# The set-up of a fused FFT and MLP-mixer kernel: sine tables by a masked scale, x folded by landed halves, and a new order with fillers on TensorE

## Chip, cores, metric

One NeuronCore of a Trainium2 chip runs the whole program. The metric is the device time of one execution in microseconds. The profile comes from one of the timed executions; its span is about 1.8 us shorter than the reported time. On one core every run counts as "fast", but the granted TensorE clock (the share of full speed that the chip allowed) differs in the set-up from run to run. Each run comes with its mean clock only. As a scale, estimated from the clock records of the traces: one stretch of 3.4 us at half clock lowers the mean by 0.0028, and a low clock at the very end of the program by up to 0.0019 more. So 0.998 to 1.000 means no low stretch in the set-up, 0.996 or 0.997 one, 0.993 or 0.994 two, 0.990 to 0.992 three.

## The reference

```python
def reference(x, w_tok1, w_tok2, w_ch1, w_ch2):      # x: 8 x 3008 x 256, float32
    x = np.fft.fft(np.fft.fft(x, axis=1), axis=2).real
    xt = x.transpose(0, 2, 1)
    h = np.maximum(xt @ w_tok1, 0.0) @ w_tok2        # token MLP, width 256
    u = x + h.transpose(0, 2, 1)
    h2 = np.maximum(u @ w_ch1, 0.0) @ w_ch2          # channel MLP, width 1536
    return u + h2
```

## The kernel before

The kernel builds its own sine tables while the first batch of x loads. For batch 0 the order of work is: fold x with its mirror (`xm`, two gathers) on VectorE; products `pz` with a small sine table and their copies `z`; products `pw` with the feature table `tdu`/`tdb` and their copies `w`; the token tables `tp` and `tq` are made by ScalarE sines, turned on TensorE (`tts_p`, `tts_q`) and multiplied into the token weights w1 (`ph` products, copies `hp` and `hq`). Then the token MLP of batch 0 and the main stage follow; I call its first channel product (`pc`) the start of the main stage.

The token weights are loaded after x on the same queue:

```python
    x_tiles = {0: load_x(0)}          # four loads of xp, two gathers of xm
    ...
    for i in range(2):
        gdma(w1p[64 * i:64 * i + 64, :, :],
             dram(w1_t, i * DTOK, [[NQ * DTOK, 64], [2 * DTOK, NG], [1, DTOK]]))
        gdma(w1m[64 - 64 * i:128 - 64 * i, 0:NG - 1 + i, :],
             dram(w1_t, (25 - i) * DTOK,
                  [[NQ * DTOK, 64], [2 * DTOK, NG - 1 + i], [1, DTOK]]))
    w2s = const.tile([P, 2, S], FP16, tag="w2s")
    gdma(w2s[:], ...)
```

The tables, the `ph` products, and the order of the set-up:

```python
    def table3(tab, r):                     # tab: 128 x 12 x 128; two quarters of it stay zero
        for i in range(2):
            h = slice(64 * i, 64 * i + 64)
            sin(tab[h, :, h], r[h, :, :], S)

    def carried(tts, dst, g2, e):           # two groups of 12; needs w1p[g] and w1m[11 - g]
        ph = ps_mm("ph")
        for k in range(2):
            g = 2 * g2 + k
            o = ph[:, k * DTOK:(k + 1) * DTOK]
            nc.tensor.matmul(o, lhsT=tts[0][...], rhs=w1p[:, g, :], start=True, stop=False)
            nc.tensor.matmul(o, lhsT=tts[1][...], rhs=w1m[:, NG - 1 - g, :], ...)
        copy(e, dst[...], ph[:])
    ...
    warm(36)                    # warm-up matmuls, 256 columns
    turn(tp, tts_p, 0)          # 12 transposes; the last argument counts filler matmuls (result unused)
    pieces = fold0()
    take(pieces, 1)
    table_d()
    table_perm()
    take(pieces, 4)
    own = zw0()                 # steps: 8 of pz, then 12 of pw
    ...                         # rest of vq on VectorE
    take(own, 3)
    turn_rows(tts_p, 1.0, 0)
    table_b()
    take(own, 5)
    table3(tq, vq)
    take(own, 3)
    carried(tts_p, hp, 0, 1)    # first use of w1
    ...                         # the other pw, five more hp, tq turned
```

## Time and profile before

| | before |
|---|---|
| time, median of 3 | 611.73 us (611.49 to 612.89) |
| run that was profiled | 612.39 us, span 610.6 us, mean clock 0.991 |
| start of the main stage in that run | 39.50 us |

From the page of the profile: span, TensorE's busy time, the granted clock in 40 slices of 15 us (tenths of full speed), and the engines' shares of the chain that ended last.

```profile
span 610.6 us, 15693 instructions
...
PE 594.0 (97%) x6319; PEld 425.0 (70%) x6319; DVE 453.7 (74%) x1017; ACT 441.0 (72%) x988; POOL 147.9 (24%) x232
...
PEclk9699999999999999999999999999999999999999
...
PE 92%; DVE 4%; DMA 1%; ACT 1%; issue 0%; POOL 0%; DVEq 0%; POOLq 0%
...
```

TensorE bounds the kernel, and only the second slice of 40 shows a clock below 90%. The windows view (busy us of each engine and number of instructions, then the granted clock, a share of the DMA engines that I don't use, and GB/s) cuts the set-up into stretches of 3.4 us:

```profile
core 0: us, PE busy (x) PEld busy (x) DVE busy (x) ACT busy (x) POOL busy (x), PEclk, DMA share, GB/s
9.20:12.60 3.40, 1.98 (x19) 1.53 (x18) 2.06 (x8) 3.25 (x6) 2.88 (x5) 1.00 1.10 186
12.60:16.00 3.40, 1.24 (x22) 1.07 (x22) 2.68 (x9) 2.02 (x4) 1.48 (x2) 1.00 1.43 192
16.00:19.40 3.40, 3.40 (x33) 2.13 (x30) 3.40 (x8) 3.00 (x6) 3.23 (x6) 0.50 1.47 198
19.40:22.80 3.40, 2.94 (x24) 2.27 (x22) 2.36 (x6) 2.13 (x4) 2.95 (x9) 0.50 1.14 221
22.80:26.20 3.40, 3.40 (x31) 3.13 (x29) 1.33 (x3) 1.50 (x3) 2.71 (x5) 0.50 1.07 221
...
```

In the stretch before 16.0 us TensorE is busy for 1.24 of 3.40 us; then the clock is 0.50 for three stretches. (The clock's records in a trace begin at its first rise, here at 9.2 us. The views count the time before as full, but the warm-up matmuls of 256 columns start 0.21 us apart in it and 0.11 us apart after it.) From the chain of waits (start, us, what):

```profile
...
5.27 7.93 DMA xm<-in_x_dram,ix
...
15.58 0.40 PE pz L476 x5
...
18.78 1.67 DVE z L293 x3
...
20.50 1.38 PE pw L519 x11
21.88 0.21 PE ph L398
...
39.50 1.42 PE pc L704 x6
...
```

The fold starts when the second gather lands (13.2 us), z is done at 20.45. From the timeline (start, us from the first start to the last end of the merged instructions, engine, instruction, count; in brackets the idle time and what ended it):

```profile
...
3.90 1.67 ACT L140 ACTIVATE tp<-pcol 64x768 f16<-64x768 f32 x2
...
5.58 1.69 ACT L140 ACTIVATE tq<-pcol 64x768 f16<-64x768 f32 x2
...
10.85 1.68 ACT L245 ACTIVATE tp<-vp 64x768 f16<-64x768 f32 x2
...
13.32 0.23 DVE L447 TENSOR_TENSOR xp<-xp,xm 94x16 f16<-94x16 f16 x1 [1.99 <-DMA xm<-in_x_dram,ix]
...
15.07 2.74 POOL L90 TENSOR_SCALAR tdu<-tdu 128x1 f16<-128x1 f16 x2 [1.92 <-ACT tdu L245]
...
21.68 0.42 PE L398 MATMUL ph<-w1p,tt 128*128 128x256 f16 x1
...
21.89 0.42 PE L400 MATMUL ph<-w1m,tt 128*128 128x256 f16 x1
...
```

Four zero fills occupy ScalarE for 3.4 us; the fold waits 1.99 us for the gather; two tiny steps on GpSimd take 2.74 us.

### The profile page before, as it was taken

To read this page: it belongs to the slowest core of one execution; us is meant where nothing else is said; L and a number is where in the kernel's file an instruction comes from. 1 tells how busy PE (TensorE), PEld (TensorE's weight loads), DVE (VectorE), ACT (ScalarE), POOL (GpSimd) and SP (SyncE) were. 2 spreads that over 40 slices of the span, in tenths; PEclk is the share of its full clock that TensorE was granted. 3 is DMA by queue.
4 is the path that set the end of the run, shared out by engine and by line. 5 is a ranking of instruction groups with operands and counts; after the bars stand their busy time and mean duration, and the time that the engine had idled before them with its cause. 6 is when DMAs were issued, how large, how long until landed. Compare 5 with 4: busy or idle time off the path is not lost.

```text
span 610.6 us, 15693 instructions
## 1 busy us (share of the span) xinstructions
PE 594.0 (97%) x6319; PEld 425.0 (70%) x6319; DVE 453.7 (74%) x1017; ACT 441.0 (72%) x988; POOL 147.9 (24%) x232
## 2 busy tenths in 40 slices
PE   4999999999999999999999999999999999999996
PEld 3765667666777677766777777766777667766675
DVE  7669679658987598757988689856979676676572
ACT  8667887686778777777777767777777777767772
POOL 7700413211233112401414211321121112111131
PEclk9699999999999999999999999999999999999999
DMA  9993943824538423682339233383231523342424
GB/s 148 209 178 87 176 83 56 160 44 84 74 66 155 96 53 62 115 131 53 71 70 167 62 77 80 63 184 61 53 66 44 103 53 75 66 70 58 91 58 100
DMA packets 86601, 56.53 MB, mean 93 GB/s; under 512 B 54864, under 2 KB 83472, under 8 KB 85776
## 3 DMA queue, kind: packets, MB, share of 16 engines
q1 hardware_dynamic: 78048, 37.84, 32.5%
q0 software_dynamic: 8256, 17.49, 16.5%
q8 instruction: 49, 0.80, 0.6%
q14 instruction: 24, 0.20, 0.1%
q10 hardware_dynamic: 224, 0.20, 0.1%
HBM read 34.98 MB, written 24.64 MB: 98 GB/s over the span
## 4 chain that ended last, share of the span: by engine, by line
PE 92%; DVE 4%; DMA 1%; ACT 1%; issue 0%; POOL 0%; DVEq 0%; POOLq 0%
PE pc L704 39%; PE px L745 23%; PE py L745 9%; PE pu L664 7%; PE po L802 4%; PE pt L572 4%; PE pz L476 2%; DMA xm<-in_x_dram,ix 1%; PE pq L604 1%; PE py L604 1%; PE pw L519 1%; PE pw L556 1%; DVE sb L721 1%; PE pw L555 1%; DVE w L558 1%; PE ph L400 1%
## 5 line engine op out<-in xcount | busy, mean ns | idle before, releaser
L707 ACT ACTIVATE c<-pc 128x512 f16<-128x512 f32 (+1 forms) x572 | 295.9, 595 | 38.5 <-PE pc L704 20.5
L730 POOL TENSOR_TENSOR osb<-osb,rt 128x256 f32<-128x256 f32 x84 | 80.1, 954 | 384.4 <-DVE osb L730 374.5
L704 PE MATMUL pc<-ut,wc1p 128*128 128x512 f16 x576 | 140.5, 379 | 0.0
L745 PEld LDWEIGHTS <-c 128*128 128x128 f16 x2016 | 121.4, 98 | 20.8 <-issue 1.2
L704 PE MATMUL pc<-ut,wc1m 128*128 128x512 f16 (+1 forms) x576 | 134.9, 370 | 0.0
L672 DVE TENSOR_TENSOR ut<-pu,yt 128x512 f16<-128x512 f32 (+1 forms) x96 | 64.6, 674 | 52.9 <-PE pu L664 52.8
L745 PEld LDWEIGHTS <-sb 128*128 128x128 f16 x1512 | 90.0, 98 | 10.8 <-DVE sb L721 0.7
L750 ACT ACTIVATE m<-px 128x256 f32<-128x256 f32 x126 | 48.5, 385 | 66.6 <-PE px L745 42.9
L704 PEld LDWEIGHTS <-wc1p 128*128 128x128 f16 x576 | 52.1, 98 | 49.2 <-issue 2.6
L704 PEld LDWEIGHTS <-wc1m 128*128 128x128 f16 x576 | 53.0, 98 | 46.4
L745 PE MATMUL px<-wst,c 128*128 128x128 f16 x1008 | 70.8, 219 | 0.2 <-DVE c L721 0.2
L745 PE MATMUL px<-wc,c 128*128 128x128 f16 x1008 | 63.1, 219 | 0.0
L295 ACT ACTIVATE z<-pz 128x480 f16<-128x480 f32 (+1 forms) x59 | 39.7, 673 | 17.7 <-PE pz L476 11.9
L721 DVE TENSOR_TENSOR sb<-sb,c 128x768 f16<-128x768 f16 x84 | 50.3, 598 | 2.9
L730 DVE TENSOR_TENSOR osb<-py,m 128x256 f32<-128x256 f32 x84 | 35.1, 418 | 22.2 <-ACT m L750 17.4
L664 PE MATMUL pu<-w2p,uu 128*128 128x512 f16 (+1 forms) x168 | 50.0, 379 | 0.0
L721 DVE TENSOR_TENSOR sb<-c 128x768 f16<-128x768 f16 x84 | 48.1, 573 | 2.4 <-ACT c L707 2.4
L721 DVE TENSOR_TENSOR sb<-c,sb 128x768 f16<-128x768 f16 x84 | 47.1, 561 | 0.0
L721 DVE TENSOR_TENSOR c<-c 128x768 f16<-128x768 f16 x84 | 46.5, 554 | 0.0
L558 DVE SCALAR_TENSOR_TENSOR w<-alt,pw 128x131 f16<-128x131 f16 x84 | 29.3, 350 | 19.7 <-ACT w L295 19.1
L611 DVE TENSOR_TENSOR yt<-py,qs 128x512 f16<-128x512 f32 x48 | 30.9, 686 | 16.1 <-ACT qs L607 15.8
L745 PE MATMUL py<-wst,sb 128*128 128x128 f16 x504 | 35.2, 219 | 0.5 <-DVE sb L721 0.5
(187 smaller groups left out, 696.2 us busy)
## 6 DMA issues: line engine op xcount, KB each, us to landing
out_dram<-osb SPq DMA_DIRECT2D x83, 256.0 KB, 3.8
xp<-in_x_dram POOLq DMA_DIRECT2D x16, 272.0 KB
out_dram<-osb SPq DMA_DIRECT2D x11, 192.0 KB, 3.2
xp<-in_x_dram POOLq DMA_DIRECT2D x16, 127.5 KB
rt<-ut SPq DMA_TRANSPOSE x96, 3.5
w2s<-in_moe_w_tok_dram POOLq DMA_DIRECT2D x1, 1504.0 KB
w1p<-in_moe_w_tok_dram POOLq DMA_DIRECT2D x2, 384.0 KB
wc<-in_moe_w_ch_dram POOLq DMA_DIRECT2D x1, 768.0 KB
```

What stands on the lines that cost most here:

```text
L295: nc.scalar.activation(out=out_, in_=in_, func=AFT.Copy)
L558: nc.vector.scalar_tensor_tensor(out=w[:, g, 0:131], in0=alt[:], scalar=pw[:, 131:132], in1=pw[:, 0:131], op0=AT.mult, op1=AT.add)
L572: nc.tensor.matmul(pt[:, o:o + n], lhsT=hw[:, g, th * P:th * P + P], rhs=w[:, g, f:f + n], start=(g == 0), stop=(g == NG - 1))
L611: nc.vector.tensor_tensor(out=yt[:, h, CW * c:CW * c + CW], in0=py[:], in1=qs[:], op=op)
L664: nc.tensor.matmul(pu[:, 0:n], lhsT=uu[:, th, int(minus), h, :], rhs=w2_cols(b, c)[:, th], start=(th == 0), stop=(th == 1))
L672: nc.vector.tensor_tensor(out=ut[:, h, 0:n].rearrange("p (a b) -> p a b", b=64), in0=pu[:, 0:n].rearrange("p (b a) -> p a b", b=64), in1=y ...
L704: nc.tensor.matmul(pc[:, 0:n], lhsT=wc[:, h, ct * P:(ct + 1) * P], rhs=ut[:, h, 0:n], start=(h == 0), stop=(h == 1))
L707: nc.scalar.activation(out=c1[:, ct, 0:n], in_=pc[:, 0:n], func=AFT.Relu)
L721: nc.vector.tensor_tensor(out=o, in0=x, in1=y, op=op)
L730: eng.tensor_tensor(out=o, in0=x, in1=y, op=AT.add)
L745: nc.tensor.matmul(o[:, t], lhsT=a(k)[:, f:f + P], rhs=w(k), start=(first and t == 0 and k == 0), stop=(k == HC - 1), skip_group_check=True)
L750: nc.scalar.activation(out=m[:, i], in_=pa[:, 0], func=AFT.Copy)
```

## The change

Its intent: the quarters of tp and tq that must be zero come out of the sine itself, by a scale vector that is 0 on half the partitions; rounding for vp goes from VectorE to ScalarE and the two tiny steps from GpSimd to VectorE; the first half of the fold needs only the first gather; and the order on TensorE, with more fillers, should leave no idle spell long enough to halve the clock.

```diff
-    for t in (tp, tq):
-        for i in range(2):
-            h = slice(64 * i, 64 * i + 64)
-            nc.scalar.activation(
-                out=t[h, :, 64 - 64 * i:128 - 64 * i],
-                in_=pcol[h, :].unsqueeze(2).to_broadcast([64, NG, 64]),
-                func=AFT.Copy, scale=0.0)
...
     def table3(tab, r):
         for i in range(2):
-            h = slice(64 * i, 64 * i + 64)
-            sin(tab[h, :, h], r[h, :, :], S)
+            nc.scalar.activation(out=tab[:, :, 64 * i:64 * i + 64], in_=r[:],
+                                 func=AFT.Sin, scale=half[i][:])
...
+    near(vp, mp)
+    half = pvec("half0"), pvec("half1")
+    ts(half[0][:], icol[:], -PI2 / S, AT.mult, PI2 / S, AT.add)
+    ts(half[1][:], icol[:], PI2 / S, AT.mult)
...
-        tt(out=xp[:, 1:NR, 0], in0=xp[:, 1:NR, 0], in1=xm[0:KR, ::-1, 0], op=add)
...
+        for t0 in (13, 9, 5, 1):
+            if t0 in (13, 5):
+                mirror(t0 - 4, t0 + 4, 0, 1)
+            mirror(t0, t0 + 4, 1, D)
...
-    Z0_ORDER = ((11, (0, 1)), (0, (1, 1)), (6, (0, 1)), (1, (0, 1)))
-    W0_COPY = [1] * 5 + [0, 1, 0, 1, 0, 1, 0]
+    Z0_ORDER = ((11, (0, 0)), (0, (1, 1)), (6, (0, 1)), (1, (0, 1)))
+    W0_COPY = [1] * 5 + [0, 1, 1, 1, 0, 1, 0]
...
-    warm(36)
-    turn(tp, tts_p, 0)
+    warm(24)
+    near(vq, mq)
+    table_d()
     pieces = fold0()
-    take(pieces, 1)
...
+    take(pieces, 5)
+    own = zw0()
+    filler(8)
+    take(own, 2)
+    turn(tp, tts_p, 8)
+    take(own, 2)
+    table_b()
+    rest_of(vq, mq, S)
+    take(own, 4)
+    turn_rows(tts_p, 1.0, 0)
+    table3(tq, vq)
     table_perm()
...
     take(own, 3)
     carried(tts_p, hp, 0, 1)
```

More of the change, by code (lines that the diff above doesn't have):

```diff
@@ L285, in filler @@
     def filler(n):
-        pw = ps_out("filler")
+        pw = ps_mm("filler")
         for _ in range(n):
@@ L307 @@
     ts(gp[:], jrow[:, 0:NG], r2[:], AT.mult, offp[:], AT.add)
-    nc.vector.memset(altu[:], 1.0)
-    for f in (2, 132):
-        nc.vector.memset(altu[:, f:f + 127:2], -1.0)
     nc.vector.scalar_tensor_tensor(
@@ L314, with near, rest_of @@
         op0=AT.mult, op1=AT.add)
-    ixc = const.tile([P, 1], I32, tag="ixc")
-    cfeat = pvec("cfeat")
-    ts(cfeat[:], pcol[:], 1.0, AT.is_lt, -128.0, AT.mult)
-    ts(cfeat[:], cfeat[:], 256.0, AT.add)
-    nc.vector.tensor_tensor(out=ixc[:], in0=cfeat[:], in1=pcol[:], op=AT.subtract)
-    for o, i, scale, bias in ((mq, mp, 1.0, dq), (vq, mq, 1.0 / S, up),
-                              (vq, vq, 1.0, down)):
-        nc.scalar.activation(out=o[:], in_=i[:], func=AFT.Identity, scale=scale,
-                             bias=bias[:])
+    nc.vector.memset(altu[:], 1.0)
+    for f in (2, 132):
+        nc.vector.memset(altu[:, f:f + 127:2], -1.0)
+    def near(v, m):
+        for i, scale, bias in ((m, 1.0 / S, up), (v, 1.0, down)):
+            nc.scalar.activation(out=v[:], in_=i[:], func=AFT.Identity, scale=scale,
+                                 bias=bias[:])
+    def rest_of(v, m, period):
+        nc.vector.scalar_tensor_tensor(out=v[:], in0=v[:], scalar=-float(period),
+                                       in1=m[:], op0=AT.mult, op1=AT.add)
+    near(vp, mp)
+    half = pvec("half0"), pvec("half1")
+    ts(half[0][:], icol[:], -PI2 / S, AT.mult, PI2 / S, AT.add)
+    ts(half[1][:], icol[:], PI2 / S, AT.mult)
     mask0, q24 = pvec("mask0"), pvec("q24")
@@ L338 @@
     nc.scalar.activation(out=t0h[:], in_=cs[0:NQ, 0:4:2, :], func=AFT.Copy, scale=0.5)
-    reduced(vp[:], vp[:], mp[:], S)
+    rest_of(vp, mp, S)
     table3(tp, vp)
+    nc.scalar.activation(out=mq[:], in_=mp[:], func=AFT.Identity, bias=dq[:])
     ident = const.tile([P, P], FP16, tag="ident")
@@ L351 @@
     nc.vector.tensor_copy(out=t1b[:, 0:3:2, :], in_=t1n[:, :, 0, :])
+    ixc = const.tile([P, 1], I32, tag="ixc")
+    cfeat = pvec("cfeat")
+    ts(cfeat[:], pcol[:], 1.0, AT.is_lt, -128.0, AT.mult)
+    ts(cfeat[:], cfeat[:], 256.0, AT.add)
+    nc.vector.tensor_tensor(out=ixc[:], in0=cfeat[:], in1=pcol[:], op=AT.subtract)
+    nc.vector.scalar_tensor_tensor(out=md[:], in0=vd[:], scalar=-256.0, in1=md[:],
+                                   op0=AT.mult, op1=AT.add)
     td0 = const.tile([P, 131], FP16, tag="td0")
@@ L358, in table_d, with table_b @@
     def table_d():
-        nc.vector.scalar_tensor_tensor(out=md[:], in0=vd[:], scalar=-256.0, in1=md[:],
-                                       op0=AT.mult, op1=AT.add)
         sin(tdu[:, 2:130], md[:, 0:128], 256)
         sin(tdu[:, 132:WD], md[:, 128:255], 256)
+    def table_b():
         for f, s in ((1, 0.5), (130, -0.5)):
-            ts(tdu[:, f:f + 1], tdu[:, 129:130], 0.5, AT.mult, s, AT.add, eng=pl)
-    def table_b():
+            ts(tdu[:, f:f + 1], tdu[:, 129:130], 0.5, AT.mult, s, AT.add)
         nc.vector.tensor_tensor(out=tdb[:], in0=tdu[:], in1=altu[:], op=AT.mult)
@@ L446, in fold0, with mirror @@
         tt, add = nc.vector.tensor_tensor, AT.add
-        tt(out=xp[:, 1:NR, 0], in0=xp[:, 1:NR, 0], in1=xm[0:KR, ::-1, 0], op=add)
+        def mirror(t0, t1, lo, hi):
+            rv = slice(16 - t0, 16 - t1 if t1 < 17 else None, -1)
+            rd = slice(D - lo, D - hi if lo else None, -1) if lo else 0
+            c = slice(lo, hi) if lo else 0
+            t = slice(t0, t1)
+            tt(out=xp[:, t, c], in0=xp[:, t, c], in1=xm[0:KR, rv, rd], op=add)
         r = slice(0, NQ)
-        for t0, t1 in ((13, 17), (9, 13), (5, 9), (1, 5)):
-            t = slice(t0, t1)
-            rv = slice(16 - t0, 16 - t1 if t1 < 17 else None, -1)
-            tt(out=xp[:, t, 1:D], in0=xp[:, t, 1:D], in1=xm[0:KR, rv, D - 1:0:-1], op=add)
+        for t0 in (13, 9, 5, 1):
+            if t0 in (13, 5):
+                mirror(t0 - 4, t0 + 4, 0, 1)
+            mirror(t0, t0 + 4, 1, D)
             yield
@@ L840, in take @@
             next(g, None)
-    warm(36)
-    turn(tp, tts_p, 0)
+    warm(24)
+    near(vq, mq)
+    table_d()
     pieces = fold0()
-    take(pieces, 1)
-    table_d()
-    table_perm()
-    take(pieces, 4)
-    own = zw0()
-    nc.vector.scalar_tensor_tensor(out=vq[:], in0=vq[:], scalar=-float(S), in1=mq[:],
-                                   op0=AT.mult, op1=AT.add)
-    take(own, 3)
-    turn_rows(tts_p, 1.0, 0)
-    table_b()
-    take(own, 5)
-    table3(tq, vq)
+    take(pieces, 5)
[9 more added lines that the diff above has]
+    table3(tq, vq)
+    table_perm()
     take(own, 3)
@@ L860 @@
     carried(tts_p, hp, 1, 0)
-    take(own, 1)
+    take(own, 2)
+    carried(tts_p, hp, 2, 1)
     turn(tq, tts_q, 0)
     take(own, 2)
-    carried(tts_p, hp, 2, 1)
+    carried(tts_p, hp, 3, 1)
     turn_rows(tts_q, -1.0, 0)
-    take(own, 2)
-    carried(tts_p, hp, 3, 1)
-    take(own, 2)
+    take(own, 3)
     carried(tts_p, hp, 4, 0)
```

## The prediction

> **What bounds it now.** The page shows TensorE busy 97% of 610.6 us, and the chain of waits is 92% TensorE. The change touches only the set-up, the first 31 us; later work keeps its order on every engine, so at most the start of the main stage (first channel product, 39.5 us in the chain) moves. The chain of set-up: the second gather of mirrored x lands at 13.2 us; VectorE folds x in four blocks until 16.7; casts of z end at 20.45, and the first full run of pw products starts at 20.50; from there TensorE, with copies to VectorE and ScalarE, sets the pace to 31 us.
>
> The windows view gives the granted clock: 1.00 until 16.0, 0.50 from 16.0 to 26.2, then 1.00. Before the drop TensorE was busy only 1.25 of 3.41 us (idle 1.42 us before the transposes of tp and 2.16 us before pz). The Trainium skill, "TensorE: Matmul & The Clock Gate", Part 1, says that a free-running window of about 3.4 us decides the clock. This trace fits: half speed lasts 10.2 us, three windows. In the halved stretch a pw matmul of 128 columns starts every 0.11 us, later every 0.056.
>
> **What the change does.**
> - Removes four ScalarE zero fills (0.84 us each, 3.36 in all). The sines grow from 64 to 128 partitions at the same 768 columns, so 0.84 us each as before.
> - Moves two passes of vp (0.55 + 0.69 us) from VectorE to ScalarE (two of 0.94), and two tiny GpSimd steps (1.4 us each) to VectorE (0.15 each, estimate).
> - Folds the first two blocks after the first gather alone. The gathers are issued 1.7 us apart; I estimate it lands near 11.2 us. Fold ends near 14.8 instead of 16.7.
> - Puts pz before the tp transposes, defers the reversed rows and the tq sines, adds 16 filler matmuls, and takes 12 of 36 warm-up matmuls away, which also start 0.95 us later (mp comes first).
>
> By hand, with the trace's durations: tdu sines end 14.0; first pz 13.4; z complete near 19.1, against 20.45. Gain 1.3 us. Then the first ph product may wait for w1, which lands near 21 us (w2s, next in the queue, lands at 28.4 after about 7.5 us of bytes). If the clock is full there, 2.9 us of halved matmul time goes away, but the copies take over: about 5.5 us each on VectorE and ScalarE after 21 us, so the last hp copy ends near 27.3, against 30.8 to 31.3. All set-up gain passes to the end, because w2s (28.4) and wc1 land before they are needed.
>
> So: clock full, about -3.5 us; clock halved again, about -1.3. The second is a real chance: I expect TensorE idle from 10.6 to 13.4, and again about 1.4 us before pw, and 24 cold warm-up matmuls (0.213 us each, 5.1 us) need not fill one free-running window. I give full clock two chances in three.
>
> **Predicted: 608.7 us**, range 606.8 to 610.6 (before 611.73). Faster by over 2% 1%, within 2% 98.5%, slower 0.5%.
>
> **What would show it.** Windows view: granted clock 1.00 from 16 to 26 us. Timeline: first fold near 11.2 with the releaser a DMA, first pz near 13.4, z done near 19, last hp copy near 27.3. Main stage of unchanged length, starting near 36 instead of 39.5. ScalarE's fills absent.
>
> **What would make it wrong.** The two gathers landing together at 13.2 (the fold then gains nothing); the clock halving at 12.6 or 16 after all, or never rising after the shorter warm-up; w1 landing later than 21 us; ScalarE, which now has the vq passes and the tdu sines just before the z copies, becoming the bound; or loads of the next batch colliding differently and giving the gain back at the first channel products.

## The result

| | before | changed |
|---|---|---|
| time, median of 4 | 611.81 us (611.49 to 612.89) | 612.26 us (611.57 to 612.66) |
| ratio of fast runs | | 1.0003 (0.9986 to 1.002) |
| profiled run | 612.39 us, span 610.6 | 611.57 us, span 609.8 |
| start of the main stage | 39.50 us | 38.72 us |

Ratios here and below are the mean time of one kernel's fast runs over that of the other's of the same rounds, so they are not quite the ratio of the medians. The predicted 3 us did not come, and the measured median lies above the predicted range. The profiled run of before is one of its slower ones, that of the changed kernel is its fastest of four, so the 0.8 us between the two profiles is no gain of the medians.

The page of the changed kernel:

```profile
span 609.8 us, 15701 instructions
...
PEclk9899999999999999999999999999999999999999
...
```

The windows view, the same stretches:

```profile
...
9.20:12.60 3.40, 2.56 (x19) 1.82 (x17) 3.33 (x16) 3.33 (x5) 3.10 (x4) 1.00 1.14 197
12.60:16.00 3.40, 3.15 (x57) 2.86 (x58) 2.51 (x8) 3.40 (x8) 3.04 (x6) 1.00 1.45 195
16.00:19.40 3.40, 1.68 (x16) 0.93 (x15) 2.92 (x6) 3.40 (x7) 2.98 (x7) 1.00 1.51 208
19.40:22.80 3.40, 1.25 (x10) 0.97 (x9) 0.99 (x3) 0.80 (x1) 2.50 (x5) 0.78 1.07 214
22.80:26.20 3.40, 3.40 (x39) 3.09 (x38) 2.16 (x5) 1.31 (x3) 0.00 (x0) 0.72 1.05 218
...
```

The recorded clock is now full from its first rise (11.1 us) until 21.3 us. But TensorE is busy for only 1.68 us and 1.25 us of the third and fourth stretch, and the clock then falls after all. The chain of waits says why:

```profile
...
8.68 12.91 DMA w1m<-in_moe_w_tok_dram
...
21.64 0.37 PE ph L403
22.01 0.21 PE ph L401
...
38.72 1.42 PE pc L714 x6
...
```

The gather of x and the fold have left the chain, and so have z and the first pw products. In their place stands one line of 12.91 us: the load of w1m, from its issue to its landing at 21.6 us. The timeline shows the same on TensorE:

```profile
...
8.71 1.76 ACT L242 ACTIVATE tp<-vp,half 128x768 f16<-128x768 f32 x2 [0.29 <-DVE vp L315]
...
10.95 0.77 DVE L456 TENSOR_TENSOR xp<-xp,xm 94x8 f16<-94x8 f16 x2
...
12.85 0.60 PE L486 MATMUL pz<-t1n,xp 94*128 94x96 f16 x10 [1.09 <-DVE xp L456]
...
15.53 0.39 DVE L90 TENSOR_SCALAR tdu<-tdu 128x1 f16<-128x1 f16 x2
...
19.22 0.27 PE L401 MATMUL ph<-w1p,tt 128*128 128x256 f16 x1
...
21.64 0.37 PE L403 MATMUL ph<-w1m,tt 128*128 128x256 f16 x1 [2.15 <-DMA w1m<-in_moe_w_tok_dram]
...
```

The pieces of the change did as intended: no zero fills, sines on 128 partitions at 1.76 us for two (1.68 on 64), the fold starts at 10.95 without a wait instead of 13.32, the first pz is at 12.85 instead of 15.58. "ScalarE: Activation LUTs", Step-by-step, in the Trainium skill states that scale may be a per-partition operand. A single sine took 0.93 to 0.97 us with it on 128 partitions, against 0.83 with one scale for all on 64; the prediction had 0.84 "as before". What each of the two differences costs was not separated. The first product with w1p starts at 19.22, 2.5 us earlier than before. The next instruction needs w1m and waits 2.15 us; TensorE takes its instructions in order, so all the later pw products, which need nothing more, stand behind it. The first w1m product starts at 21.64, against 21.89 before: a gain of 0.25 us. And behind the wait the clock is low: the chain has 0.21 us for each `ph` product, where at full clock it has 0.11.

From the start of the main stage to the end the two kernels take the same: 610.6 - 39.5 = 571.1 and 609.8 - 38.7 = 571.1 us. In all the runs below this lies between 570.9 and 571.3 (in halves_w_first_filled the chain does not pass the first pc; by its start on TensorE, 35.05, it is 571.4), so the start of the main stage tells a profiled run's worth, and the loss must be looked for in front of it.

### The profile page after: what moved, and what is told of

It reads as the page before. It is cut to its first block, busy times and chain, and to the rows that moved or that the text cites. A ratio compares the mean times of both kernels' runs of the same rounds, so it can differ in the third digit from the quotient of the medians.

```text
span 609.8 us, 15701 instructions
## 1 busy us (share of the span) xinstructions
PE 591.3 (97%) x6323; PEld 423.0 (69%) x6323; DVE 453.2 (74%) x1020; ACT 439.4 (72%) x986; POOL 147.8 (24%) x230
## 4 chain that ended last, share of the span: by engine, by line
PE 92%; DVE 3%; DMA 2%; ACT 1%; POOL 1%; issue 0%; DVEq 0%; POOLq 0%
PE pc L714 39%; PE px L755 23%; PE py L755 9%; PE pu L674 7%; PE po L812 4%; PE pt L582 4%; DMA w1m<-in_moe_w_tok_dram 2%; PE pz L486 1%; PE pq L614 1%; PE py L614 1%; PE pw L566 1%; PE pw L565 1%; DVE sb L731 1%; DVE w L568 1%; PE ph L403 0%; DVE osb L740 0%
## 5 line engine op out<-in xcount | busy, mean ns | idle before, releaser
L288 ACT ACTIVATE z<-pz 128x480 f16<-128x480 f32 (+1 forms) x60 | 40.0, 671 | 16.9 <-PE pz L486 11.0
L621 DVE TENSOR_TENSOR yt<-py,qs 128x512 f16<-128x512 f32 x48 | 30.9, 686 | 16.0 <-ACT qs L617 15.7
```

Source lines behind the costliest of these rows:

```text
L288: nc.scalar.activation(out=out_, in_=in_, func=AFT.Copy)
L621: nc.vector.tensor_tensor(out=yt[:, h, CW * c:CW * c + CW], in0=py[:], in1=qs[:], op=op)
```

## The experiments

Theory A: the change shortens the way to the first w1 product, but w1m lands at 21.6 us whatever the engines do. Before was already within about 0.3 us of that landing (if w1m landed then as in the changed kernel: its own trace shows no wait, so it only says that the load was in by 21.89, and in before_filled below it came later). The wait takes the gain, and the idle in it halves the clock of the work behind it. Rivals: the copies on VectorE and ScalarE bound this stretch (B); the order of the loads matters, but cutting them costs as much as it gains (C); or the change itself is worth nothing (D).

Every run below was correct and is compared with the kernel before, run beside it on the same chip (medians 611.36 to 611.44 us there).

### w_first: nothing that needs w1 in front of pw

```diff
-    take(own, 3)
-    carried(tts_p, hp, 0, 1)
-    take(own, 2)
-    carried(tts_p, hp, 1, 0)
-    ...
+    take(own, 7)
+    turn(tq, tts_q, 0)
+    take(own, 2)
+    turn_rows(tts_q, -1.0, 0)
+    take(own, 3)
+    for g2, e in ((0, 1), (1, 0), (2, 1), (3, 1), (4, 0), (5, 1)):
+        carried(tts_p, hp, g2, e)
```

> The changed kernel, with all pw products and the tq transposes put before the six hp products, so that nothing on TensorE waits for w1 at 19 us. Theory A (the gain was lost to the wait for the w1m load, which lands at 21.6 us whatever the engines do, and to the halved clock that the wait brings): no wait for w1m over 0.5 us, the main stage starts at about 35 us instead of 38.7, the time is 3 to 4 us under the changed kernel. Rival B (the copies on VectorE and ScalarE bound this stretch, so the order does not matter): within 1 us of the changed kernel.

Measured: 608.91 us (608.49 to 611.38), ratio 0.9956 (0.9943 to 0.9969). The wait for w1m is gone, as the timeline of its profiled run shows:

```profile
...
26.46 0.27 PE L401 MATMUL ph<-w1p,tt 128*128 128x256 f16 x1
26.57 0.27 PE L403 MATMUL ph<-w1m,tt 128*128 128x256 f16 x1
...
```

B falls: the same copies, in another order, allow a shorter time. The gain over the kernel before is 2.5 us, over the changed kernel about 3. It was run at another time. The expected main stage start of 35 us was not in the profile (38.30), because the profiled run was this kernel's slowest: 611.38 us at mean clock 0.993, where the five others took 608.5 to 609.3 at 0.998 to 1.000. In its trace the clock is low twice, for 3.4 us from 13.4 and from 20.2 us. Same program, same chip: the clock's state goes with 2 to 3 us. The Trainium skill, "TensorE: Matmul & The Clock Gate", Part 1, says that the clock is set by a free-running window of 4096 cycles, 3413 ns, and that the place of the transition varies from run to run. The low stretches in the traces last 3.4, 6.8 and 10.2 us, and the first rise lies between 8.3 and 11.1 us.

### w1_halves: the needed half of w1 first

```diff
-    for i in range(2):
-        gdma(w1p[64 * i:64 * i + 64, :, :], ...)
-        gdma(w1m[64 - 64 * i:128 - 64 * i, 0:NG - 1 + i, :], ...)
+    for k in range(2):
+        for i in range(2):
+            a, n = 6 * k, 6
+            gdma(w1p[64 * i:64 * i + 64, a:a + n, :], ...)
+            a, n = (0, 6) if k else (6, 5 + i)
+            gdma(w1m[64 - 64 * i:128 - 64 * i, a:a + n, :], ...)
```

> The changed kernel, with each of the four w1 loads cut in two over the groups, and the halves that the first three hp products need put in front: same bytes, four more transfers. Theory A: the first ph product finds its weights (landing estimated at 18 us), its wait for w1m goes from 2.15 us to under 0.3, the clock stays at 1.00 from 19 to 25 us, and the time is 2.5 to 4 us under the changed kernel. Rival B (copies bound it): within 1 us. Rival C (the order of the loads costs GpSimd time and delays later loads): slower.

Measured: 608.42 us (607.27 to 611.09), ratio 0.9952 (0.9931 to 0.9973): 2.9 us under before, with the same bytes and four more transfers. The `ph` products start without a wait. C falls. The clock part of the expectation held only partly: in the profiled run (609.90 us) it was full from 17 us on, but halved for 3.4 us before that. The runs again order by mean clock: 607.3 to 607.8 at 0.998 or above, 609.1 to 611.1 below.

### filled_wait: the wait stays, the clock is held

```diff
     take(own, 3)
+    filler(36)
     carried(tts_p, hp, 0, 1)
```

> The changed kernel with 36 filler matmuls in TensorE's wait before the first ph product (19.2 to 21.6 us; 2.0 us of work at full clock). It separates the wait from the clock: the landing of w1m stays at 21.6. If the halved clock from 21.2 to 24.6 is what costs, the granted clock is 1.00 throughout and the time falls by 1 to 1.7 us. If the wait alone and the copies behind it cost, the time falls by under 0.5 us.

Measured: 610.84 us (610.12 to 611.67), ratio 0.9992 (0.9977 to 1.0007). In three of six runs the clock was 0.998 or above and the time 610.12 to 610.26; in the three others it was 0.997 and the time 611.42 to 611.67. The profiled run is of the first kind. Its timeline on TensorE:

```profile
...
19.24 2.17 PE L281 MATMUL filler<-ident 128*128 128x128 f16 x36
...
21.59 0.27 PE L403 MATMUL ph<-w1m,tt 128*128 128x256 f16 x1
21.70 0.27 PE L401 MATMUL ph<-w1p,tt 128*128 128x256 f16 x1
...
```

The fillers occupy the wait, w1m lands no earlier (21.59), and the work behind runs at 0.11 us per `ph` product. The main stage starts at 37.19 instead of 38.72: holding the clock behind the wait is worth 1.5 us between these two profiled runs. By medians it is 1.4 us against the first four runs of the changed kernel, so the clock is a real part of the loss. They were run at other times. But even with full clock the kernel is only 1.2 us under before: the landing of w1m is the other part.

### before_filled: the kernel before with its clock held

```diff
-    turn(tp, tts_p, 0)
+    turn(tp, tts_p, 24)
```

> The kernel before with 24 filler matmuls after the tp transposes (the idle 13.4 to 15.6 us), nothing else: it undoes the halved clock alone, without the landed halves and the masked scale. If the clock holds at 1.00 past 16 us, theory A says that the w1m landing at 21.6 us caps the gain before it, and that the rest to 26 us runs at full clock: 1 to 2.5 us faster than the kernel before. If the halved clock was harmless (work waited for VectorE anyhow): within 0.5 us.

Measured: 612.81 us (611.26 to 613.39), ratio 1.0017 (1.0002 to 1.0033). I had expected a gain of 1 to 2.5 us or none; it was slightly slower. The clock held past 16 us, as meant, and pw started earlier. Then the timeline shows:

```profile
...
21.49 0.42 PE L398 MATMUL ph<-w1p,tt 128*128 128x256 f16 x1
22.37 0.37 PE L400 MATMUL ph<-w1m,tt 128*128 128x256 f16 x1 [0.47 <-DMA w1m<-in_moe_w_tok_dram]
...
```

The kernel before, brought forward only a little, runs into the same load, which in this run landed at about 22.3 us. The clock fell at about 20 us instead of 16 and stayed low for 6.8 us, now over the work behind the load. So the half clock of the kernel before looks harmless in part: it fell in a stretch that waited for VectorE and for w1 anyhow, and moving it later moved it to where it costs.

### after_again and before_w1_halves: the same load cut, with and without the change

The first is the changed kernel unaltered, the second is the kernel before with the cut w1 loads shown above.

> The changed kernel unaltered, timed again beside the others of this call. Expected under theory A (w1m landing caps it; the clock falls in the wait behind it in some runs): within 1 us of the kernel before, mean clock 0.994 to 0.998 run by run, the slower runs those with the lower mean clock.

> The kernel before with the cut w1 loads only. Its own first ph product came at 21.7 us, after z was done at 20.45 and at halved clock, so it hardly waited for w1m. Theory A says that the cut loads alone give it little: within 0.8 us of the kernel before. If the cut loads give it the same 3 us as they gave the changed kernel, then the change itself brings nothing and the loads everything (rival D).

Measured: after_again 612.04 us (610.27 to 613.00), ratio 1.0011 (0.9998 to 1.0025). before_w1_halves 611.93 us (611.06 to 612.97), ratio 1.0005 (0.9992 to 1.0018). Rival D falls. The cut loads alone give the kernel before nothing, the change alone gives nothing, and both together give 2.9 us. That is what two limits that happen to stand side by side look like: whichever is moved, the other holds.

In none of the ten timed runs of the changed kernel was the mean clock above 0.996. The expected order of time by mean clock held loosely (610.27 and 611.67 both at 0.996, 611.09 at 0.993): it counts where the half clock falls. In the fastest run (610.27 us) the trace shows it from about 13.4 to 16.9 us, TensorE reached w1m just as it landed (a wait of 0.22 us), and the main stage started at 37.27.

### halves_filled: cut loads and enough fillers

```diff
-    filler(8)
+    filler(24)
     take(own, 2)
...
-    turn_rows(tts_p, 1.0, 0)
+    turn_rows(tts_p, 1.0, 16)
     table3(tq, vq)
```

(on top of w1_halves)

> The changed kernel with cut w1 loads, 24 instead of 8 fillers after the warm-up and 16 fillers after the reversed rows, to hold the clock through the idle spells at 11 to 13 and 16 to 18 us. If the spread of w1_halves (605.5 to 609.3 us span) is the clock window's phase, the mean clock is 0.998 or above in every run, and the time is 607 to 608 us with a spread under 1.5. If fillers delay real work instead: above w1_halves' fast runs by up to 1 us with full clock.

Measured: 607.78 us (607.60 to 607.91), ratio 0.9938 (0.9925 to 0.9951); five runs in 0.3 us, all at mean clock 0.998 or above. This is the fastest version by median, 3.7 us under before; the runs of w1_halves at full clock, 607.27 to 607.75, are as fast, so what the extra fillers bring is that every run holds the clock. Windows view and timeline:

```profile
...
12.60:16.00 3.40, 2.87 (x54) 2.67 (x55) 2.60 (x8) 3.38 (x8) 1.97 (x3) 1.00 1.44 194
16.00:19.40 3.40, 2.62 (x37) 1.94 (x35) 2.83 (x8) 3.40 (x8) 2.57 (x5) 1.00 1.49 203
19.40:22.80 3.40, 3.40 (x53) 3.26 (x50) 3.19 (x9) 2.35 (x5) 2.95 (x9) 1.00 1.09 217
22.80:26.20 3.40, 3.09 (x33) 2.26 (x31) 1.73 (x4) 3.40 (x8) 2.69 (x5) 1.00 1.08 223
...
```

```profile
...
11.22 0.77 DVE L459 TENSOR_TENSOR xp<-xp,xm 94x8 f16<-94x8 f16 x2 [0.68 <-DMA xm<-in_x_dram,ix]
...
13.03 0.49 ACT L241 ACTIVATE tdu<-md 128x128 f16<-128x128 f32 x2
...
13.55 1.09 ACT L291 ACTIVATE z<-pz 128x480 f16<-128x480 f32 x2
...
19.41 0.27 PE L404 MATMUL ph<-w1p,tt 128*128 128x256 f16 x1
...
19.52 0.27 PE L406 MATMUL ph<-w1m,tt 128*128 128x256 f16 x1
...
```

The granted clock is 1.00 in every stretch, the first `ph` products come at 19.41 and 19.52 without a wait, and the main stage starts at 35.12 us. In this trace the first two pieces of w1m, which the first products need, had landed by 16.9 us and the last piece at 21.6, where the uncut load landed. The starts of the main stage now add up, with one traced run each: 38.72 (changed) to 37.19 (filled_wait) is the clock, 1.5 us; 37.19 to 35.12 (halves_filled) is the load, 2.1 us.

### halves_whole_fold: the landed halves undone

```diff
-            if t0 in (13, 5):
-                mirror(t0 - 4, t0 + 4, 0, 1)
+            if t0 == 13:
+                mirror(1, NR, 0, 1)
```

(on top of w1_halves)

> The changed kernel with cut w1 loads, but with the fold's first step waiting for both gathers of x as in the kernel before (landed halves undone). The landed halves start the fold 2 us earlier (11.0 or 11.5 against 13.3 us); if that is on the critical path once w1 is no longer the cap, this run is 1 to 2.2 us slower than w1_halves at the same clock; if ScalarE (vq passes and sines until 14 us) is the bound there, under 0.5.

Measured: 610.94 us (608.95 to 612.07), ratio 0.9989 (0.9972 to 1.0007). At mean clock 1.000 it takes 608.95 us against 607.75 for w1_halves, 1.2 us, with one run on each side; the medians differ by 2.5 us, and the clock was low more often (0.990 to 0.997 in five of six runs). They were run at other times. In the profiled run it fell at 15.7 us, after the wait for the second gather (the fold starts at 13.20). So the landed halves are on the critical path once w1 is not the cap, and ScalarE alone does not bound the start of z.

### filled_zero_fills: the masked scale undone

(halves_filled with the four fills and the old `table3` back, as in the lines marked - of the change.)

> halves_filled (changed kernel, cut w1 loads, more fillers) with the masked scale undone: the four zero fills (3.4 us of ScalarE) and the half-partition sines are back. In halves_filled ScalarE is busy without a break from 12.6 to 19.4 us. If ScalarE is the bound there, the tdu sines and the z copies come about 1.8 us later (fills end at 7.3 instead of 5.5, when the vp passes could start) and the time rises by 1 to 2 us. If not, within 0.4.

Measured: 609.46 us (609.43 to 609.76), ratio 0.9965 (0.9951 to 0.998): 1.7 us more than halves_filled (the kernel before took 611.40 and 611.44 us), with the clock held in both. They were run at other times. ScalarE's timeline:

```profile
...
3.89 1.68 ACT L140 ACTIVATE tp<-pcol 64x768 f16<-64x768 f32 x2
5.58 1.69 ACT L140 ACTIVATE tq<-pcol 64x768 f16<-64x768 f32 x2
...
15.03 0.50 ACT L248 ACTIVATE tdu<-md 128x128 f16<-128x128 f32 x2
15.43 1.05 ACT L298 ACTIVATE z<-pz 128x480 f16<-128x480 f32 x2
...
```

With the fills the sines of tdu start at 15.03 and the first z copies at 15.43, against 13.03 and 13.55 in halves_filled. The masked scale is worth 1.7 us here, where w1 comes in time and the clock is held; in front of a late w1 it was not tested alone.

### before_halves_filled: both caps lifted for the kernel before

(The kernel before with the cut loads, 24 fillers after the tp transposes and 16 after the reversed rows.)

> The kernel before with both caps lifted: cut w1 loads, 24 fillers after the tp transposes and 16 after the reversed rows to hold the clock. If the new order, the landed halves and the masked scale have a worth of their own, it stays 1.5 to 3 us slower than halves_filled, and is 0.5 to 2 us faster than the kernel before. If the caps were everything, it comes within 0.7 us of halves_filled.

Measured: 609.65 us (609.31 to 611.67), ratio 0.9973 (0.9955 to 0.9991). So about half of the 3.7 us between before and halves_filled comes from lifting the caps (1.8 us), and half is the change's own (1.9 us: 609.65 to 607.78). They were run at other times. In this pair both sides have cut loads and a held clock, so it is the fair price of the change. The parts do not add up: undoing the masked scale alone costs 1.7 us and undoing the landed halves alone 1.2, each with the other in place, and the whole change is worth 1.9.

### halves_w_first_filled: order again, with the caps gone

(halves_filled with the order of w_first.)

> halves_filled with the pw products and the tq transposes put before all hp products. With the w1 cap gone, the order should not matter for the wait; if finishing w and the tq turn early frees the chain of ScalarE copies (tt of tq), up to 1 us faster than halves_filled; if hp copies then pile up before the token product, up to 1 us slower.

Measured: 608.20 us (608.10 to 608.39), ratio 0.9944 (0.9929 to 0.9958), 0.4 us slower than halves_filled in median. It was run at another time. The order that was worth about 3 us against a late w1 is worth nothing when w1 is there in time.

## Why the prediction was wrong, point by point

- **Folding by halves, masked scale, pz before the transposes.** Right in mechanism. Predicted: first fold near 11.2, first pz near 13.4, tdu sines done at 14.0, z complete near 19.1. In the changed kernel: 10.95, 12.85, 13.63, and z complete at 18.5.
- **The load of w1. This is the step that failed.** The prediction has "Then the first ph product may wait for w1, which lands near 21 us", and then adds up the gain as if this wait took nothing. It lands at 21.59, the first product that needs it starts at 21.64, and the kernel before first used w1m at 21.89. So with w1m landing there, no order of the earlier work could bring that use forward by more than 0.25 us; the 1.3 us of an earlier z could not pass through. I read 21.68 and 21.89 in the trace of before, saw that no wait stood there, and did not compare them with the estimated landing. A wait of zero does not mean a distance: w1 had about a quarter of a microsecond of slack if it landed as in the changed kernel, and in before_filled, which wanted it at 21.7, none.
- **"clock halved again, about -1.3".** This term should have been about 0: with w1m fixed at 21.6 and half clock behind it, the order of work after that point is nearly that of before. Measured: +0.5 and +0.6 us in the two medians of the changed kernel, with intervals that include 0.
- **"clock full, about -3.5".** Mis-sized for the kernel as changed: filled_wait's runs at clock 0.998 or above are 1.2 us under before. The last hp copy was predicted to end near 27.3; there it ended at 28.99, and in halves_filled at 26.93. The 3.5 is what the change with both caps lifted gives (3.7).
- **"full clock two chances in three".** Wrong: none of ten runs. I feared the idle at 10.6 to 13.4 and before pw; in the profiled run the clock survived those and fell in the wait for w1m, which I had listed under what would go wrong only as a later landing. In the traced run of after_again it did fall behind the first of these, at 13.4 us.
- **The base.** The profile of before that I costed from was a slow run (612.39 us, clock 0.991 with 10.2 us at half speed). Its faster runs have 0.993, so part of the "2.9 us of halved matmul time" was not in the median to be gained.
- **Main stage of unchanged length**: right, 571.1 us in both.

What stays open: why w1m landed at 21.6 us in one run and at 22.3 in another (one difference: GpSimd issued the last w1 load at 9.5 us in before and before_filled and at 8.7 us in the changed kernel, so the change moved that load a little too; that this moved the landing is not shown); where the half clock fell in the eight runs of the changed kernel that were timed without a trace, for which only the mean clock is known; and how busy a clock window must be, which the busy time of the profile does not tell (below).

## What to carry to other kernels

Before costing a shorter path, list for every input of the first product behind it when its load lands, and how much slack the present use has; an input used without a wait may have landed just before. When a change and its limit are suspected to hide each other, run both alone and together: here 0, 0 and -2.9 us. On an in-order TensorE put work that needs nothing in front of work that waits for a load, and fill what idle is left, because the halved clock is paid after the wait, not in it.

## What the Trainium skill lacked or had wrong

- In "TensorE: Matmul & The Clock Gate", Part 1, the table of the two states puts the fall after at least one idle window. Here a window does not have to be idle: in before the clock fell after 3.4 us with TensorE busy for 1.24 us of them, in the changed kernel after 3.41 us (17.91 to 21.32) with 0.91 us. Nor does the busy time that the profile shows give a limit, if the windows lie as the falls suggest: the clock fell after 3.41 us with 1.86 us busy in w_first (16.81 to 20.22) and 2.04 us in before_filled (16.57 to 19.98), and held after 1.82 us in halves_whole_fold (8.85 to 12.26) and 1.98 us in before (9.2 to 12.6). It does not tell the rise either: in before TensorE was busy throughout the first low window, and the clock stayed low for two more.
- The same part puts the penalty of the ramp at the start below 1% of a typical span and advises not to fit to a count of cold matmuls. The later fall here is below 1% too, but for a change worth 0.6% of the span it was of the size of the effect: 1.5 us from one 3.4 us stretch at half clock behind a wait.
- "DMA: Bandwidth & Descriptors", SWDGE vs HWDGE vs iDMA, says that a load that casts must be issued from GpSimd. The loads of x and of the weights cast float32 to FP16 and are all issued there, so w1 stands in one queue behind x; no page says how to place a load by its first use within such a queue. Cutting it in two and putting the needed half first cost no time to be seen here (all of w1m in at 21.6 us either way) and was worth 3.6 us to the changed kernel (612.04 to 608.42 us). They were run at other times.
